# Splitting the first loads of a LayerNorm-MLP kernel over two DMA queues, and the first copy into two parts

## Chip, cores and metric

The kernel runs on 1 core of a Trainium2 chip. The metric is device time in microseconds for one execution of the whole program. Before the change three runs gave 396.62, 396.86 and 396.88 us; the median is 396.86 us.

## What is computed

```python
def _layernorm(x, axis=-1, eps=1e-5):
    m = jnp.mean(x, axis=axis, keepdims=True)
    v = jnp.var(x, axis=axis, keepdims=True)
    return (x - m) / jnp.sqrt(v + eps)

# B, S, D, F = 1, 2048, 1024, 3584; all inputs bfloat16
def reference(x, w1, b1, w2, b2):
    y = _layernorm(x, axis=-1)
    h = _gelu(jnp.einsum("bsd,df->bsf", y, w1) + b1)     # tanh approximation
    return jnp.einsum("bsf,fd->bsd", h, w2) + b2
```

## The kernel before

The 2048 rows of `x` are cut into 16 tiles of 128 rows, and four tiles make a block of 512 rows. For each block the kernel needs the normalized rows transposed (`yT_sb`, with the 1024 features in 8 groups of 128), then multiplies by `w1` (28 rows of 128 hidden features, 8 matmuls each), applies gelu on ScalarE into `hT_sb`, multiplies by `w2` and adds `b2` on VectorE. Blocks 1 to 3 are normalized and transposed on VectorE while TensorE works on the block before them.

Block 0 has nothing ahead of it to hide behind, so it is treated differently. Its first three tiles (`N_RAW = 3`) are transposed raw, that is, not yet normalized, by TensorE (`pe_T`, line 378): four transposes of 128x128 per half tile go to a PSUM bank, and ScalarE copies the bank to `yT_sb` (line 386). TensorE multiplies these raw values by the first 7 rows of `w1` (`cells`, through `pe_cell`, line 410), in the order that is written out by hand at lines 560 to 591: an order that follows the arrival of the loads. Meanwhile VectorE computes the statistics of each half tile (`op_stats`, line 269), from them the mean and the reciprocal deviation; these are turned into rows and spread over the partitions by GpSimd (line 497). VectorE then shifts the raw copies for the later rows of `w1` (`ops_fix`, line 334) and corrects the products of the first 7 rows in PSUM (lines 537 and 540). Only after that can ScalarE apply the first gelu and hand back the first PSUM bank to TensorE. Tile 3 is normalized before it is transposed (line 294).

VectorE's statistics run in a fixed order: first halves of tiles 0, 1, 2, then their second halves, then tile 3. The engines run separate instruction streams, each in the order in which the code puts it, and wait for one another by semaphores.

Ahead of all this TensorE does 24 dummy matmuls (`WARM`, line 486), and ScalarE loads the table for the square root (line 489).

The loads are issued from two queues. In the names of the first loads, `x0a` is the first half (512 columns) of tile 0; `xrb` is one transfer with the second halves of tiles 0 to 2 (384 KB); `w0` to `w7` are chunks of `w1` with 128 of the 1024 input features and the first 896 hidden features each (224 KB). ScalarE's queue carries `x1a` and `x2a`; all others are on SP's queue, in the order of `SP_FIRST_LOADS` (line 26). After the first loads SP issues the rest of `w1`, block 1 of `x`, `w2`, `b2` and the last two blocks.

Of the kernel before, what the change touches and what calls it, by code (L numbers as in the profile page):

```python
# [5 lines left out]
ACT = mybir.ActivationFunctionType  # L6
# [7 lines left out]
TPB = TB // P  # L14
# [5 lines left out]
WARM = 24  # L20
N_RAW = 3
RC = N_RAW * P
HALVES = (0, 4, 8)
W1_CHUNK_COLS = (512, 512, 1024, 640)
N_W2_CHUNKS = 4
SP_FIRST_LOADS = ("x0a", "w0", "w1", "w2", "xrb", "w3", "w4", "x3a", "x3b", "w5", "w6", "w7", "b1", "w8")
ACT_FIRST_LOADS = ("x1a", "x2a")

T_PE_START = 4.2
T_DVE_START = 26.0  # L30
# [54 lines left out]
def bass_standalone__mixer_channel_mlp__prompt_kernel(  # L85
# [13 lines left out]
    DT = D // P  # L99
# [6 lines left out]
    assert HC <= 512 and DT * P * 2 <= 2048 and FT >= 4 and FT <= P  # L106
    R = max(1, min(R_WAVE, FT - 2, NB1 + NB2))
    assert NB1 + NB2 + 1 <= 8 and NB2 == 2
    assert HALVES[-1] == DT and 0 < N_RAW < TPB

    w1_chunks = [(j, j + 1, 0, R * P) for j in range(DT)]
    c0 = R * P
# [24 lines left out]
    with ExitStack() as es:  # L137
# [34 lines left out]
        act = _Prog("s_act")  # L172
# [7 lines left out]
        x_ev = {}  # L180
        w1_issued = set()

        def dma(dst, src, sig, nbytes, waits=()):
            dma_q[0].op(lambda e, dst=dst, src=src: e.dma_start(dst, src), waits=waits, sig=sig, sem="d_" + sig, inc=16)
            dma_bytes[0] += nbytes
            est[sig] = DMA_T0 + dma_bytes[0] / DMA_BYTES_PER_US

        def load_x_tile(i):
            dma(x_sb[:, i, :], xf[i * P:(i + 1) * P, :], f"x{i}", P * D * 2)
            x_ev[i] = (f"x{i}", f"x{i}")  # L190
# [7 lines left out]
        def load_w1(ci):  # L198
            j0, j1, a, b = w1_chunks[ci]
            dma(w1_sb[:, j0:j1, a:b], w1v[:, j0:j1, a:b], f"w1c{ci}", (j1 - j0) * P * (b - a) * 2)  # L200
            w1_issued.add(ci)
# [5 lines left out]
        def issue(item):  # L207
            if item == "xrb":
                dma(x_sb[:, 0:N_RAW, HC:D], xf[0:N_RAW * P, HC:D].rearrange("(t p) d -> p t d", p=P), item,
                    N_RAW * P * HC * 2)  # L210
                for i in range(N_RAW):
                    x_ev[i] = (f"x{i}_0", item)
            elif item[0] == "x" and item[-1] in "ab":
                i, h = int(item[1:-1]), "ab".index(item[-1])
                dma(x_sb[:, i, h * HC:(h + 1) * HC], xf[i * P:(i + 1) * P, h * HC:(h + 1) * HC], f"x{i}_{h}",
                    P * HC * 2)
                x_ev[i] = (f"x{i}_0", f"x{i}_1")
            elif item == "b1":
                b1v = b1.rearrange("(t q a) -> q t a", q=4, a=32)
                for q in range(4):  # L220
                    dma(b1r_sb[32 * q:32 * q + FT, :], b1v[q], f"b1{q}", F // 2, waits=["b1z"])
            elif item[0] == "x":
                load_x_tile(int(item[1:]))
            elif item[0] == "w" and int(item[1:]) < len(w1_chunks):
                load_w1(int(item[1:]))

        dma_q[0] = act
        for item in ACT_FIRST_LOADS:
            issue(item)
        dma_q[0] = sp  # L230
        for item in SP_FIRST_LOADS:
            issue(item)
        for i in range(TPB):
            if i not in x_ev:
                load_x_tile(i)
            else:
                for h, evn in enumerate(x_ev[i]):
                    if evn not in est:
                        issue(f"x{i}" + "ab"[h])
# [10 lines left out]
        for b in range(2, NB):  # L250
# [5 lines left out]
                waits=["ones"], sig="ident")  # L256
# [11 lines left out]
        def op_stats(i, h):  # L268
            return (lambda e, i=i, h=h: e.bn_stats(st_sb[:, i, 6 * h:6 * (h + 1)], x_sb[:, i, h * HC:(h + 1) * HC]),  # L269
                    [x_ev[i][h]], f"st{i}_{h}", 0.65)  # L270

        def op_aggr(i):
            if i >= TPB:
                pool.op(lambda e, i=i: e.tensor_tensor(out=rstd_sb[:, i:i + 1], in0=mv_sb[:, i, 1:2],  # L274
                                                       in1=nhalf[:, i:i + 1], op=ALU.pow),
                        waits=[f"mv{i}", "nhalf"], sig=f"rstd{i}")
            return (lambda e, i=i: e.bn_aggr(mv_sb[:, i, :], st_sb[:, i, :]),  # L277
                    [f"st{i}_0", f"st{i}_1", "eps"], f"mv{i}", 0.33)
# [20 lines left out]
        y_ev = {}  # L299
# [32 lines left out]
        def ops_fix(i):  # L332
            s0, s1 = i * P, (i + 1) * P
            return [(lambda e: e.tensor_tensor(out=yT_sb[:, 0, :, s0:s1], in0=yT_sb[:, 1, :, s0:s1],  # L334
                                               in1=row_sb[:, 0:1, s0:s1].to_broadcast([P, DT, P]), op=ALU.add),
                     ["row0", f"te{i}_0", f"te{i}_1"], f"fx{i}v", 1.25)]

        yT_ev = {}
        mm1_done = {}
# [19 lines left out]
        def dve_put(o):  # L359
            dve.op(o[0], waits=o[1], sig=o[2])  # L360
# [4 lines left out]

        def pe_T(parts, bname):
            bap = t_bank[bname]
            nb = HALVES[1]
            last = f"tp{parts[-1][0]}_{parts[-1][1]}"
            w0 = ["ident"] + ([bank_read[bname]] if bname in bank_read else [])  # L370
            copies = []
            for n, (i, k) in enumerate(parts):
                j0, j1 = HALVES[k], HALVES[k + 1]
                buf, s0 = (1 if i < N_RAW else 0), i * P
                o = n * nb * P
                for j in range(j0, j1):
                    waits = (w0 if n == 0 else []) + [x_ev[i][k] if i < N_RAW else y_ev[i][j]] if j == j0 else []
                    pe.op(lambda e, i=i, j=j, o=o + (j - j0) * P: e.transpose(  # L378
                        out=bap[:, o:o + P], in_=x_sb[:, i, j * P:(j + 1) * P], identity=ident[:, :]),
                        waits=waits, sig=(f"tp{i}_{k}" if j == j1 - 1 else None))  # L380
                    yT_ev.setdefault(i, [None] * DT)[j] = f"te{i}_{k}"
                src = bap[:, o:o + (j1 - j0) * P].rearrange("p (j s) -> p j s", j=j1 - j0)
                copies.append((yT_sb[:, buf, j0:j1, s0:s0 + P], src, f"te{i}_{k}"))
                pe_t[0] += (j1 - j0) * 0.056
            for dst, src, sig in copies:
                act.op(lambda e, dst=dst, src=src: e.copy(out=dst, in_=src), waits=[last], sig=sig)  # L386
                bank_read[bname] = sig
# [96 lines left out]
        def warm(n, gate=None):  # L484
            for _ in range(n):
                pe.op(lambda e: e.matmul(ps_1[:, 0, 0:P], lhsT=unit, rhs=unit,  # L486
                                         start=True, stop=True), waits=[gate] if gate else [])

        act.op(lambda e: e.preload_act_table(ACT.Sqrt))
        warm(WARM)  # L490
        raw = list(range(N_RAW))
        head = [op_stats(i, h) for h in range(2) for i in raw] + [op_aggr(i) for i in raw]
# [3 lines left out]
        for k in range(2):  # L496
            pool.op(lambda e, k=k: e.partition_broadcast(
                row_sb[:, k, 0:RC], rvt_sb[0:1, k * N_RAW:(k + 1) * N_RAW, :].rearrange("p v s -> p (v s)")),
                waits=["rvt", "row1c", "scr"], sig=f"row{k}")
        pool.op(lambda e: e.tensor_tensor(out=scr_sb[:, 1, :], in0=scr_sb[:, 0, :], in1=nhalf[:, :], op=ALU.pow),  # L500
                waits=["row1"])
        h = DT // 2
        FX = [f"fx{i}v" for i in raw]
        for i in raw:
            head += ops_fix(i)
        for o in head:
            dve_put(o)

# [3 lines left out]
        def cells(rows, dts, t0, t1, by_row=False):  # L512
            n0, n1 = t0 * P, t1 * P + (1 if t1 == N_RAW else 0)
            order = [(r, dt) for r in rows for dt in dts] if by_row else [(r, dt) for dt in dts for r in rows]
            for r, dt in order:
                bank = wave[r][0]
                w = [yT_ev[i][dt] for i in range(t0, t1)] + (["rone"] if n1 > RC else [])
                if r not in started:
                    w += [bank_read[k] for k in (f"{bank[0]}_{bank[1]}",) if k in bank_read]
                pe_cell(r, dt, 1, n0, n1, bank, w, f"cw_{r}" if dt == DT - 1 and n1 > RC else None,  # L520
                        r not in started, False, shared=True)
                started.add(r)
# [26 lines left out]
        def late_cells(t, rows, dts):  # L549
            for r in rows:  # L550
# [7 lines left out]
                        hT_row[(0, r)] = f"g_0_{r}"  # L558

        first, most, every = range(NB1), [*range(NB1), R - 1], range(R)  # L560
        pe_T([(0, 0)], "t")
        pe_T([(1, 0)], "2_0")
        cells(first, (0,), 0, 1)
        pe_T([(2, 0)], "2_1")
        cells(first, (0,), 1, 2)
        cells((R - 1,), (0,), 0, 2)
        cells(most, (1,), 0, 2)
# [4 lines left out]
        cells(every[4:], (2,), 0, 3)  # L572
        cells(first, (3,), 0, 3)
        pe_T([(2, 1)], "t")
        cells(every[NB1:], (3,), 0, 3)
        act.op(lambda e: e.activation(out=std_sb[:, :], in_=mv_sb[:, 0:TPB, 1], func=ACT.Sqrt, bias=0.0, scale=1.0),
               waits=[f"mv{i}" for i in range(TPB)], sig="std")
# [52 lines left out]
        while ci < len(crit) or fi < len(fill):  # L630
# [5 lines left out]
            if take_crit:  # L636
                rdy, o, _ = crit[ci]
                ci += 1
            else:
                rdy, o, _ = fill[fi]  # L640
# [46 lines left out]
```

## Time and profile before

| | before |
|---|---|
| median of 3 runs | 396.86 us (396.62 to 396.88) |
| profiled execution, its own time | 397.14 us |
| its span | 395.9 us |
| TensorE matmul busy | 393.0 us (99%) |
| VectorE busy | 160.1 us (40%) |
| ScalarE busy | 83.7 us (21%) |
| DMA, mean over the span | 60 GB/s |
| DMA, first five of the 40 slices of the span | 256 to 388 GB/s |

The span is the time from the first to the last instruction of the program in the profiled execution; the execution's own time has 1.24 us around it. In the profile PE is TensorE's matmuls, PEld its weight loads, DVE is VectorE, ACT is ScalarE, POOL is GpSimd and SP is SyncE. A name with q (ACTq, SPq) is the engine's sequencer, which issues DMAs. L386 is line 386 of the kernel. Matmul records overlap, since matmuls are pipelined: the distance of two starts says more than the length of one record. In chains of waits each piece is given with its start and its length in us; in timelines the bracket at the end gives the engine's idle time before the piece and what ended it.

### The profile page before, as it was taken

The page shows a single profiled execution, that of the slowest core. Times are in us where ns is not written, and L with a number is a line of the kernel's source. Part 1 is how long each engine was busy: PE and PEld are TensorE (multiplying, and loading weights), DVE is VectorE, ACT ScalarE, POOL GpSimd, SP SyncE. Part 2 cuts the span into 40 slices and gives each one's busy share as a digit, 9 for nine tenths or more (in the row PEclk, how much of TensorE's full clock was granted, in tenths as well). Part 3 has the DMA queues.
Part 4 walks back from the last instruction along what each step waited for, and adds up shares of the span by engine and source line. Part 5 has one row for each costly group of instructions (what it writes and reads, how often), then busy time and mean ns, then how long its engine had stood idle before and what let it go on. Part 6 is the DMA issues. An engine that isn't in the chain of part 4 may idle for free.

```text
span 395.9 us, 4579 instructions
## 1 busy us (share of the span) xinstructions
PE 393.0 (99%) x1964; PEld 186.6 (47%) x1964; DVE 160.1 (40%) x336; ACT 83.7 (21%) x125; POOL 11.9 (3%) x28
## 2 busy tenths in 40 slices
PE   8999999999999999999999999999999999999998
PEld 7744444444444444444444444444444444444445
DVE  4998889988999405987100000001100000001011
ACT  3374330000144342000023443100003334400000
POOL 0121100011000100000000000000000000000000
DMA  7999940000000000000000000000000000000000
GB/s 256 365 378 387 388 167 14 28 26 14 28 0 0 2 0 2 27 17 24 26 13 2 0 0 2 13 13 28 21 21 13 0 2 0 0 15 26 13 28 27
DMA packets 16747, 23.62 MB, mean 60 GB/s; under 512 B 1240, under 2 KB 10456, under 8 KB 16728
## 3 DMA queue, kind: packets, MB, share of 16 engines
q1 hardware_dynamic: 16440, 23.08, 16.6%
q8 instruction: 15, 0.25, 0.3%
q10 hardware_dynamic: 288, 0.26, 0.2%
q14 instruction: 4, 0.03, 0.0%
HBM read 19.14 MB, written 4.19 MB: 59 GB/s over the span
## 4 chain that ended last, share of the span: by engine, by line
PE 99%; ACT 0%; DVE 0%; issue 0%
PE ps L462 49%; PE ps L410 41%; PE ps_t L410 8%; PE ps L486 1%; PE ps_t L378 0%; ACT yT_sb L386 0%; PE ps L378 0%; DVE o_sb L473 0%
## 5 line engine op out<-in xcount | busy, mean ns | idle before, releaser
L462 PE MATMUL ps<-w_sb,hT_sb 128*128 128x512 bf16 (+2 forms) x924 | 194.1, 373 | 0.0
L410 PE MATMUL ps<-yT_sb,w_sb 128*128 128x512 bf16 (+4 forms) x832 | 167.1, 360 | 0.3 <-ACT yT_sb L386 0.3
L462 PEld LDWEIGHTS ps<-w_sb,hT_sb 128*128 128x128 bf16 x924 | 89.3, 98 | 104.5
L410 PEld LDWEIGHTS ps<-yT_sb,w_sb 128*128 128x128 bf16 x832 | 78.1, 98 | 84.8 <-ACT yT_sb L386 0.5
L419 ACT ACTIVATE hT_sb<-ps,b_sb 128x512 bf16<-128x512 f32 x94 | 64.2, 688 | 235.6 <-PE ps L410 217.2
L473 DVE TENSOR_TENSOR o_sb<-ps,b_sb 128x512 bf16<-128x512 f32 (+2 forms) x33 | 22.3, 676 | 198.5 <-PE ps L462 198.4
L354 DVE STREAM_TRANSPOSE yT_sb<-x_sb 32x256 bf16<-32x256 bf16 x192 | 83.7, 436 | 21.6 <-PE ps_t L410 18.6
L410 PE MATMUL ps_t<-yT_sb,w_sb 128*128 128x512 bf16 (+2 forms) x152 | 34.0, 368 | 0.0
L269 DVE BATCH_NORM_STATS2 st_sb<-x_sb 128x6 f32<-128x512 bf16 x32 | 21.1, 674 | 6.0 <-DMA x_sb<-in_x_dram 5.8
L410 PEld LDWEIGHTS ps_t<-yT_sb,w_sb 128*128 128x128 bf16 x152 | 14.5, 98 | 16.4
L419 ACT ACTIVATE hT_sb<-ps_t,b_sb 128x512 bf16<-128x512 f32 x18 | 12.4, 687 | 18.0 <-PE ps_t L410 14.6
L545 DVE TENSOR_TENSOR ps<-ps,row_sb 128x384 f32<-128x384 f32 x17 | 9.3, 564 | 3.1 <-PE ps L410 2.7
L274 POOL TENSOR_TENSOR rstd_sb<-mv_sb,nhalf 128x1 f32<-128x1 f32 x12 | 6.5, 542 | 99.6 <-DVE mv_sb L277 99.6
L294 DVE TENSOR_SCALAR x_sb<-x_sb,mv_sb,rstd_sb 128x1024 bf16<-128x1024 bf16 x13 | 7.0, 541 | 1.9 <-POOL rstd_sb L274 1.3
L386 ACT COPY yT_sb<-ps_t 128x512 bf16<-128x512 bf16 x6 | 3.3, 587 | 4.9 <-PE ps_t L378 4.9
L537 DVE SCALAR_TENSOR_TENSOR ps<-row_sb,cs_sb,ps 128x385 f32<-128x385 f32 x7 | 4.3, 615 | 0.0
L540 DVE TENSOR_TENSOR ps<-ps,row_sb 128x385 f32<-128x385 f32 x7 | 4.0, 568 | 0.2
L277 DVE BATCH_NORM_AGGREGATE mv_sb<-st_sb 128x2 f32<-128x15 f32 x16 | 3.3, 214 | 1.2
L334 DVE TENSOR_TENSOR yT_sb<-yT_sb,row_sb 128x1024 bf16<-128x1024 bf16 x3 | 3.7, 1293 | 0.0
L486 PE MATMUL ps<-const-bfloat16-1.0 128*128 128x128 bf16 x24 | 2.7, 312 | 0.8 <-PEq L672 0.8
L500 POOL TENSOR_TENSOR scr_sb<-scr_sb,nhalf 128x16 f32<-128x16 f32 x1 | 2.9, 2947 | 8.4 <-issue 8.4
L486 PEld LDWEIGHTS ps<-const-bfloat16-1.0 128*128 128x128 bf16 x24 | 2.5, 148 | 0.8 <-issue 0.8
(33 smaller groups left out, 18.7 us busy)
## 6 DMA issues: line engine op xcount, KB each, us to landing
w_sb<-in_w_dram SPq DMA_DIRECT2D x4, 1792.0 KB, 18.1
out_dram<-o_sb SPq DMA_DIRECT2D x31, 128.0 KB, 1.7
x_sb<-in_x_dram SPq DMA_DIRECT2D x3, 1024.0 KB, 14.0
w_sb<-in_w_dram SPq DMA_DIRECT2D x2, 1024.0 KB, 9.2
w_sb<-in_w_dram SPq DMA_DIRECT2D x1, 2048.0 KB, 15.2
w_sb<-in_w_dram SPq DMA_DIRECT2D x8, 224.0 KB, 5.7
w_sb<-in_w_dram SPq DMA_DIRECT2D x1, 1280.0 KB, 16.3
x_sb<-in_x_dram SPq DMA_DIRECT2D x3, 128.0 KB, 5.6
```

What stands on the lines that cost most here:

```text
L269: return (lambda e, i=i, h=h: e.bn_stats(st_sb[:, i, 6 * h:6 * (h + 1)], x_sb[:, i, h * HC:(h + 1) * HC]), [x_ev[i][h]], f"st{i}_{h}", 0.65)
L274: pool.op(lambda e, i=i: e.tensor_tensor(out=rstd_sb[:, i:i + 1], in0=mv_sb[:, i, 1:2], in1=nhalf[:, i:i + 1], op=ALU.pow), waits=[f"mv{i} ...
L294: return (lambda e, i=i, c0=c0, c1=c1: e.tensor_scalar(out=x_sb[:, i, c0:c1], in0=x_sb[:, i, c0:c1], scalar1=mv_sb[:, i, 0:1], scalar2=rst ...
L354: res.append((lambda e, src=src, dst=dst: e.transpose(out=dst, in_=src), waits, (f"tr{i}" if lastop else None), 0.47))
L410: pe.op(lambda e: e.matmul(unit_bank(bank)[:, n0:n1], lhsT=w1_sb[:, dt, r * P:(r + 1) * P], rhs=yT_sb[:, buf, dt, n0:n1], start=start, sto ...
L419: act.op(lambda e, r=r, n0=n0, n1=n1, bank=bank: e.activation(out=hT_sb[:, r, n0:n1], in_=unit_bank(bank)[:, n0:n1], func=ACT.Gelu_apprx_tanh,
L462: pe.op(lambda e, st=st, ft=ft, c0=c0, c1=c1, bank=bank: e.matmul(ps_2[:, bank, 0:c1 - c0], lhsT=hT_sb[:, ft, st * P:(st + 1) * P], rhs=w2 ...
L473: crit.append((est[sig], (lambda e, ob=ob, c0=c0, c1=c1, bank=bank: e.tensor_tensor(out=o_sb[:, ob, c0:c1], in0=ps_2[:, bank, 0:c1 - c0], ...
L486: pe.op(lambda e: e.matmul(ps_1[:, 0, 0:P], lhsT=unit, rhs=unit, start=True, stop=True), waits=[gate] if gate else [])
L537: return [(lambda e: e.scalar_tensor_tensor(out=ap, in0=row_sb[:, 0, :], scalar=cs_ap[r], in1=ap, op0=ALU.mult, op1=ALU.add), [f"m1_0_{r}" ...
L540: (lambda e: e.tensor_tensor(out=ap, in0=ap, in1=row_sb[:, 1, :], op=ALU.mult), [f"sa_{r}", "row1"], f"sb_{r}", 0.56)]
L545: crit.append((est[wait_ev], (lambda e: e.tensor_tensor(out=ap, in0=ap, in1=row_sb[:, 1, 0:RC], op=ALU.mult), [wait_ev, "row1"], f"sc_{r}" ...
```

## The change

Four things are edited.

1. The load `w1` (the second chunk of the weights, input features 128 to 255) and `xrb` are issued from ScalarE's queue, behind `x1a` and `x2a`, and no longer from SP's.
2. ScalarE's load of the square-root table is put behind the issue of `x1a`, ahead of the other three issues; before, it stood behind both.
3. The first half of tile 0 is transposed and copied in two parts of two transposes each (parts 2 and 3 of `PARTS`), each to a bank of its own, and the copies are 128x256 and no longer 128x512. Tiles 1 and 2 move to the next banks (`2_1` and `t`).
4. For that, the events that the copies signal are looked up by feature group, and `ops_fix` is called further down in the program text, when all copies are known; its instructions keep their place in VectorE's order.

```diff
-HALVES = (0, 4, 8)
+PARTS = ((0, 4), (4, 8), (0, 2), (2, 4))
-SP_FIRST_LOADS = ("x0a", "w0", "w1", "w2", "xrb", "w3", "w4", "x3a", "x3b", "w5", "w6", "w7", "b1", "w8")
-ACT_FIRST_LOADS = ("x1a", "x2a")
+SP_FIRST_LOADS = ("x0a", "w0", "w2", "w3", "w4", "x3a", "x3b", "w5", "w6", "w7", "b1", "w8")
+ACT_FIRST_LOADS = ("x1a", "x2a", "w1", "xrb")
...
         for item in ACT_FIRST_LOADS:
             issue(item)
+            if item == "x1a":
+                act.op(lambda e: e.preload_act_table(ACT.Sqrt))
...
-                     ["row0", f"te{i}_0", f"te{i}_1"], f"fx{i}v", 1.25)]
+                     ["row0"] + list(dict.fromkeys(yT_ev[i])), f"fx{i}v", 1.25)]
...
-                j0, j1 = HALVES[k], HALVES[k + 1]
+                j0, j1 = PARTS[k]
...
-                    waits = (w0 if n == 0 else []) + [x_ev[i][k] if i < N_RAW else y_ev[i][j]] if j == j0 else []
+                    waits = (w0 if n == 0 else []) + [x_ev[i][j // nb] if i < N_RAW else y_ev[i][j]] if j == j0 else []
...
-        act.op(lambda e: e.preload_act_table(ACT.Sqrt))
         warm(WARM)
...
-        for i in raw:
-            head += ops_fix(i)
...
-        pe_T([(0, 0)], "t")
-        pe_T([(1, 0)], "2_0")
+        pe_T([(0, 2)], "t")
+        pe_T([(0, 3)], "2_0")
+        pe_T([(1, 0)], "2_1")
         cells(first, (0,), 0, 1)
-        pe_T([(2, 0)], "2_1")
+        pe_T([(2, 0)], "t")
         cells(first, (0,), 1, 2)
...
         pe_T([(2, 1)], "t")
+        for i in raw:
+            for o in ops_fix(i):
+                dve_put(o)
```

More of the change, by code (lines that the diff above doesn't have):

```diff
@@ L108, in bass_standalone__mixer_channel_mlp__prompt_kernel @@
     assert NB1 + NB2 + 1 <= 8 and NB2 == 2
-    assert HALVES[-1] == DT and 0 < N_RAW < TPB
+    assert PARTS[1][1] == DT and 0 < N_RAW < TPB
     w1_chunks = [(j, j + 1, 0, R * P) for j in range(DT)]
@@ L216, in issue @@
                     P * HC * 2)
-                x_ev[i] = (f"x{i}_0", f"x{i}_1")
+                x_ev[i] = (f"x{i}_0", x_ev[i][1] if i in x_ev else f"x{i}_1")
             elif item == "b1":
@@ L367, in pe_T @@
             bap = t_bank[bname]
-            nb = HALVES[1]
+            nb = DT // 2
             last = f"tp{parts[-1][0]}_{parts[-1][1]}"
```

## Prediction

> **What bounds the kernel now.** I read the page first, then the chain of waits over the first microseconds, then the timeline of each engine there, and last the DMA stretch by stretch. The page:
>
> ```profile
> span 395.9 us, 4579 instructions
> ...
> PE 393.0 (99%) x1964; PEld 186.6 (47%) x1964; DVE 160.1 (40%) x336; ACT 83.7 (21%) x125; POOL 11.9 (3%) x28
> ...
> q1 hardware_dynamic: 16440, 23.08, 16.6%
> ...
> q10 hardware_dynamic: 288, 0.26, 0.2%
> ```
>
> TensorE leaves 2.9 of 395.9 us, so only the start can gain anything. q10 is ScalarE's queue: it carries just the 0.26 MB of x1a and x2a; q1 is SP's. The chain over the first 9 us:
>
> ```profile
> 0.83 2.72 PE ps L486 x24
> 3.54 0.55 PE ps_t L378 x4
> ...
> 4.12 0.59 ACT yT_sb L386
> 4.72 0.05 issue
> 4.76 0.72 PE ps L410 x5
> ...
> 8.79 0.22 PE ps_t L378 x4
> ```
>
> After the 24 warm-up matmuls come the transposes of tile 0, then the only non-TensorE link: the copy of tile 0's half, for which the first product waits. In the records of single matmuls the last transpose of x1a starts at 4.20 and, at the 107 ns of its neighbours, is through by 4.31; the first product starts at 4.76: a hole of 0.46 us. From 5.7 us on consecutive starts fit the column counts up to the end. Matmuls start 107 ns apart up to 6.05 us and 56 ns apart after it (128 columns), though the granted clock reads 1.00 throughout.
>
> A second chain runs beside TensorE, from the second halves (`xrb`) through VectorE to the first gelu:
>
> ```profile
> 8.18 1.88 DVE L269 BATCH_NORM_STATS2 st_sb<-x_sb 128x6 f32<-128x512 bf16 x3 [2.69 <-DMA x_sb<-in_x_dram]
> ...
> 11.73 0.11 DVE L281 TENSOR_SCALAR rv_sb<-mv_sb 128x3 f32<-128x3 f32 x1
> ...
> 15.19 3.73 DVE L334 TENSOR_TENSOR yT_sb<-yT_sb,row_sb 128x1024 bf16<-128x1024 bf16 x3
> 18.85 0.61 DVE L537 SCALAR_TENSOR_TENSOR ps<-row_sb,cs_sb,ps 128x385 f32<-128x385 f32 x1
> ```
>
> VectorE has idled 2.69 us for `xrb` (issued 2.64, 5.5 us to land: 8.16), and from then to the first correction it has only short gaps for ScalarE's square root (0.33) and GpSimd's broadcast. The first gelu starts at 20.09 and takes 0.69. TensorE's weight load waits for it:
>
> ```profile
> 20.83 0.14 PEld L410 LDWEIGHTS ps<-yT_sb,w_sb 128*128 128x128 bf16 x2 [0.18 <-ACT hT_sb L419]
> ```
>
> Its matmul starts at 20.87, just when the one before is through. So this chain has about 0.04 us of slack: whatever delays `xrb` by more reaches the end. The next gelus come 1.125 us apart and a row of matmuls takes 1.73, so it stalls TensorE once.
>
> Last, the DMA while both queues had work (3.28 to 4.21), and then SP's alone:
>
> ```profile
> 3.28:4.21 0.93, 0.93 (x11) 0.74 (x8) 0.82 (x2) 0.09 (x1) 0.00 (x0) 1.00 1.00 355
> 4.25:5.40 1.15, 0.90 (x10) 0.64 (x8) 1.03 (x2) 0.95 (x2) 0.00 (x0) 1.00 0.96 335
> 5.40:7.05 1.65, 1.65 (x18) 1.57 (x17) 0.09 (x1) 0.58 (x1) 0.00 (x0) 1.00 0.93 261
> ```
>
> ```profile
> q1 hardware_dynamic: 128, 0.20, 60.0%
> q10 hardware_dynamic: 139, 0.13, 39.9%
> ```
>
> The last two columns of the first are DMA share and GB/s; the second is the queues' part of 3.28 to 4.21. The engines were full (1.00), and the two queues moved about the same number of packets: they took turns.
>
> **The change, part by part.** *Copy of tile 0 in two parts.* Transposes and products stay the same in number and order. A 128x512 copy takes 0.585 us, the 128x5 copy of line 528 0.165, hence 0.83 ns per column and an estimated 0.37 us for 128x256. The copy before began 0.35 us after the start of the last transpose; two transposes earlier, this is 3.96, and its end 4.33 instead of 4.71. But the product also needs w0, which landed at 4.60, and nothing ahead of w0 moves. A transpose followed the landing of x0a (3.36) by 0.14 us, so the product starts at 4.66 to 4.74: 0.02 to 0.1 us earlier. The extra copy (two of 0.37 for one of 0.585) delays nothing: the copy of tile 1 can't start before its transposes, about 4.55, and before it started at 4.60. I count 0.03 us of gain. Banks: `2_0`, `2_1` and `t` are handed on at copies that end before their next user needs them. The fixes keep their place in VectorE's order, so moving their code costs nothing.
>
> *Table load ahead of x2a, w1 and xrb.* It takes 1.28 us, ended at 2.99 before and would end by 2.5; the first copy needs it at about 4. In this trace a sequencer runs on beside its busy engine (VectorE's takes a wait at 15.21, inside the fix that began at 15.19), so I cost the issues behind it at nothing: x2a at about 1.2, w1 at 1.7, xrb at 2.1. If they wait for it instead, each is 1.28 later (a rival below).
>
> *w1 and xrb on ScalarE's queue.* SP loses two issues of 0.47 us each, so w2, w3, w4 and x3 enter q1 earlier and lie there with data ready. From 4.25, when x2a is through, q10 holds w1 and xrb, and q1 holds w2, w3, w4, x3a, x3b. By turns:
> - w1 has 128 packets of 1792 B (0.229 MB), and as many of w2 and w3 pass beside it: 0.459 MB at 355 GB/s is 1.29 us, so the last packet at 5.54; before, 4.69. w1 lands 0.85 later, at 6.8 instead of 5.97. TensorE needs it at 6.31: a stall of about 0.5.
> - xrb has 384 packets of 1 KB, and 384 of q1 go with them: some 220 of 1792 B (rest of w3, w4), 164 of 1 KB (x3a, part of x3b). Together 0.955 MB, 2.69 us, to 8.23; before, 7.05. xrb lands 1.18 later, at 9.34.
>
> That rate is from the one stretch with the same mix, hence my choice. Ends: the best long stretch of this trace, 365 GB/s between 9.2 and 12 us and 395 in its best part, gives at 390 a delay of 0.83; xrb's own 261 GB/s, with 335 for w1, gives 2.2. A gain in landing has no row for it while turns are taken; it stands as a rival.
>
> The Trainium skill bears on this: "DMA: Bandwidth & Descriptors", section "Rules for kernel authors", says that spreading DMAs over issuing engines doesn't raise bandwidth, since all share 16 engines, and only saves issue time. Held to one-queue rows (335 and 261, a mean of 291 over 4.25 to 7.05) the delay would be about 2.1 us; the 355 of both queues lies above these but below the 365 that SP's queue reached later, so the trace doesn't contradict it.
>
> TensorE then reaches the second transposes (8.63 before, behind xrb) at about 9.1 and waits to about 9.45. VectorE starts its second halves 1.18 later, with x3 landed by then, and nothing in its chain shortens: gelu 0 ends 1.18 later, where 0.04 is slack. TensorE's stalls at w1, at the transposes and at gelu 0 are parts of this one delay and not added to it. Sum: +1.14 for xrb, -0.03 for the copy already hidden behind it: **+1.1 us**. The profiled execution took 397.14 (span 395.9 and 1.24 around it) and becomes 398.3; it lay 0.28 above the median, which becomes 396.86 + 1.14 = **398.0**.
>
> **Rivals.** *Not slower: q10 keeps its early place.* If q10's packets pass ahead of q1's backlog, w1 follows x2a at 4.25 and takes 0.64 us, and xrb takes 1.08 to 1.65 us, ending at 6.0 to 6.5: a landing 0.5 to 1 us earlier. Then the chain to gelu 0 is free, and TensorE gains at most its 0.46 us hole: 396.4 to 396.8, say 396.6. It decides from the point where xrb lands by 8.2. For it: SP's issue time of 0.47 per load is indeed saved. Against it: 128 and 139 packets in the same stretch.
>
> *The table load holds the queue.* x2a, w1 and xrb are issued 1.28 us later (2.5, 2.95, 3.4). w0, now alone, lands sooner, and x2a by turns at about 5.3 to 5.6, where TensorE wants it by 5; w1's last packet comes about 6.1 and xrb's about 8.6, since q1 has used the time: xrb 1.5 us late, 398.3. The split of the load is then not what the change says. Against it: the wait taken at 15.21.
>
> *The clock steps up late.* If holes at w1 keep the matmuls at 107 ns spacing, the 2.3 us of work between 6.31 and 8.63 takes 4.6, from 6.8 to 11.4, and TensorE is 2.8 us late: 399.6. For it: the step at 6.05 came after one hole of 0.46. Against it: the step comes before the stall at w1. The Trainium skill, "TensorE: Matmul & The Clock Gate", section "What's actually happening", lets the clock rise after one busy window and fall only after an idle one of about 3.4 us; no hole foreseen here is as long.
>
> **How the numbers follow.** By turns 0.71, q10 early 0.15, table load holding 0.10, late clock 0.04. 0.2% is 0.79 us, about what a measurement of this kernel can tell from no change. In the first case the bounds +0.8 to +2.2 give 397.6 to 399.1, and perhaps 0.08 of its 0.71 falls under the 0.79 by yet faster transfers. Of the second nearly all lies within 0.2%, since more than 0.79 us would need the step at 6.05 some 1.6 us earlier too: 0.03. Faster 0.03, same 0.20, slower 0.77. The range goes from 396.9, leaving out most of the second case, to 399.2.
>
> **What would show it.** Right: xrb lands at 9 to 10, VectorE's first second half starts there (8.18 before), TensorE idles near 6.3 and ahead of the second transposes, LDWEIGHTS waits for gelu 0, and everything from 21 us on is shifted by the same 1.1. The copies of tile 0 take 0.37, and the first product starts at 4.7, with w0. Wrong: xrb landing by 8.2, or w1 before 6.3; ScalarE's issues only from 2.5 on would point to the table load; a spacing of 107 ns beyond 7 us to the clock.

## Result and profile after

The changed kernel takes 398.57 us (median of 17 runs, 397.46 to 402.23) against 396.97 us before (17 runs beside it, 396.59 to 397.51): 1.60 us more. The ratio, estimated from all runs, is 1.0052, with a 95% interval of 1.0037 to 1.0068 (the two medians alone give 1.0040; the ratios below are estimated in the same way). The forecast was 398.0, from 396.9 to 399.2.

Single executions lie much further apart than before. Eleven of the 17 had a mean granted TensorE clock of 1.000 and took 397.46 to 398.93 us; six had 0.996 or 0.991 and took 399.70 to 402.23. The profiled one is of the second kind, the slowest of all (402.23, span 401.0); a typical one follows behind it. Its page, the lines that answer to those of before and the row of granted clock, which the page of before doesn't have:

```profile
span 401.0 us, 4581 instructions
...
PE 394.8 (98%) x1964; PEld 187.7 (47%) x1964; DVE 160.2 (40%) x336; ACT 83.8 (21%) x126; POOL 12.0 (3%) x28
...
PEclk8799999999999999999999999999999999999999
...
q1 hardware_dynamic: 15896, 22.46, 15.9%
q10 hardware_dynamic: 832, 0.88, 0.7%
```

ScalarE's queue (q10) now carries 0.88 MB. The chain of waits of the same execution over the first 26 us:

```profile
1.71 6.98 DMA w_sb<-in_w_dram
8.70 0.05 issue
8.74 4.69 PE ps L412 x26
13.43 0.85 PE ps_t L380 x8
```

w1 is issued at 1.71 and lands at 8.70; TensorE, ready for it at about 5.5, stands still. Then the products run at half rate up to about 14, and in them 8 transposes take 0.85 us where they took 0.45 before. The table by stretches (columns as before, granted clock third from the right) shows when it fell:

```profile
6.50:7.00 0.50, 0.00 (x0) 0.00 (x0) 0.00 (x0) 0.00 (x0) 0.00 (x0) 1.00 1.04 317
7.00:7.50 0.50, 0.00 (x0) 0.00 (x0) 0.00 (x0) 0.00 (x0) 0.00 (x0) 0.82 1.01 338
7.50:8.00 0.50, 0.00 (x0) 0.00 (x0) 0.00 (x0) 0.00 (x0) 0.00 (x0) 0.50 1.00 302
...
13.00:14.00 1.00, 1.00 (x10) 0.83 (x9) 1.00 (x6) 0.00 (x0) 0.00 (x0) 0.50 1.10 346
14.00:15.00 1.00, 1.00 (x9) 0.67 (x8) 1.00 (x2) 0.69 (x2) 0.00 (x0) 0.93 1.10 350
```

0.82 over 7.0 to 7.5 puts the fall at about 7.3, some 1.8 us into the hole; the clock came back shortly after 14. So about 6.8 us of this execution ran at half clock, which gives the mean of 0.991; a mean of 0.996 is, by the same sum, about 3 us at half clock.

The 16 increments of w1's semaphore, as many as the core has DMA engines (I read them as one from each), arrive in this trace between 5.78 and 6.50 us for 13 engines and at 7.70, 8.34 and 8.70 for the last three: a few late engines make the whole landing late. They were late in sending: the last of w1's 128 packets starts at 8.06 (at 5.67 in the typical execution below), and one that started at 4.55 took 1.25 us, where the median is 0.07. Why they were late is not shown.

None of the first set's executions with a clock of 1.000 has a trace. A typical execution is that of the changed kernel's second set of runs (`e5_again` below: 398.28 median; the profiled one 398.18, span 396.9). Its VectorE timeline:

```profile
9.22 1.88 DVE L271 BATCH_NORM_STATS2 st_sb<-x_sb 128x6 f32<-128x512 bf16 x3 [3.46 <-DMA x_sb<-in_x_dram]
...
12.77 0.10 DVE L283 TENSOR_SCALAR rv_sb<-mv_sb 128x3 f32<-128x3 f32 x1
...
16.23 3.73 DVE L336 TENSOR_TENSOR yT_sb<-yT_sb,row_sb 128x1024 bf16<-128x1024 bf16 x3
19.88 0.61 DVE L536 SCALAR_TENSOR_TENSOR ps<-row_sb,cs_sb,ps 128x385 f32<-128x385 f32 x1
```

and the weight load that waits for the first gelu:

```profile
21.87 1.19 PEld L412 LDWEIGHTS ps<-yT_sb,w_sb 128*128 128x128 bf16 x7 [0.60 <-ACT hT_sb L421]
```

Every entry of VectorE's chain stands 1.03 to 1.04 us later than before (8.18, 11.73, 15.19, 18.85), the gelu ends at 21.82 instead of 20.78, and the span is 1.04 longer. All that this execution lost is the lateness of `xrb`.

### The profile page after: what moved, and what is told of

It is laid out like the page before. It is cut to its first block, busy times and chain, and to the rows that moved or that the text cites. A ratio compares the mean times of both kernels' runs of the same rounds, so it can differ in the third digit from the quotient of the medians.

```text
span 401.0 us, 4581 instructions
## 1 busy us (share of the span) xinstructions
PE 394.8 (98%) x1964; PEld 187.7 (47%) x1964; DVE 160.2 (40%) x336; ACT 83.8 (21%) x126; POOL 12.0 (3%) x28
## 3 DMA queue, kind: packets, MB, share of 16 engines
q1 hardware_dynamic: 15896, 22.46, 15.9%
## 4 chain that ended last, share of the span: by engine, by line
PE 97%; DMA 2%; ACT 0%; ACTq 0%; DVE 0%; issue 0%
PE ps L464 48%; PE ps L412 41%; PE ps_t L412 8%; DMA w_sb<-in_w_dram 2%; PE ps_t L380 0%; ACT L231 0%; ACTq L184 0%; DVE o_sb L475 0%
## 5 line engine op out<-in xcount | busy, mean ns | idle before, releaser
L412 PE MATMUL ps<-yT_sb,w_sb 128*128 128x512 bf16 (+4 forms) x832 | 169.0, 363 | 3.5 <-DMA w_sb<-in_w_dram 3.5
L412 PEld LDWEIGHTS ps<-yT_sb,w_sb 128*128 128x128 bf16 x832 | 79.0, 100 | 88.7 <-DMA w_sb<-in_w_dram 3.3
L388 ACT COPY yT_sb<-ps_t 128x512 bf16<-128x512 bf16 (+1 forms) x7 | 3.7, 557 | 11.1 <-PE ps_t L380 11.1
```

The costliest lines, as they stand in the source:

```text
L412: pe.op(lambda e: e.matmul(unit_bank(bank)[:, n0:n1], lhsT=w1_sb[:, dt, r * P:(r + 1) * P], rhs=yT_sb[:, buf, dt, n0:n1], start=start, sto ...
```

## Experiments

All differences lie within a few us at the start, so for most I give the landings of w1 and xrb in the profiled execution beside the time. A landing is one execution's; two tables at the end of this section put them side by side. Only differences from the changed kernel or the one before are shown.

**Only the split copy** (loads and table load as before):

```diff
-SP_FIRST_LOADS = ("x0a", "w0", "w2", "w3", "w4", ...
+SP_FIRST_LOADS = ("x0a", "w0", "w1", "w2", "xrb", "w3", "w4", ...
-ACT_FIRST_LOADS = ("x1a", "x2a", "w1", "xrb")
+ACT_FIRST_LOADS = ("x1a", "x2a")
-            if item == "x1a":
+            if item == "x2a":
```

> Only the copy of tile 0 in two parts; all loads and the table load as before the change. Theory (taking turns: the loss is all in the loads): xrb lands at about 8.2 us as before, the copies of tile 0 take 0.37 us each, the first product starts at 4.65 to 4.74 instead of 4.76, held by w0; time within 0.1 us of 396.97. Rival (the split copy itself costs, by one more ScalarE instruction and other banks): slower by 0.3 us or more with xrb unmoved.

Measured: 396.89 against 397.04 us, ratio 0.9995 (0.9986 to 1.0004): no difference. A line each of the timelines of ScalarE, of TensorE's matmuls and of its weight loads:

```profile
3.79 0.37 ACT L388 COPY yT_sb<-ps_t 128x256 bf16<-128x256 bf16 x1 [0.81 <-PE ps_t L380]
```

```profile
4.72 0.44 PE L412 MATMUL ps<-yT_sb,w_sb 128*128 128x128 bf16 x5 [0.63 <-DMA w_sb<-in_w_dram]
```

```profile
20.53 0.55 PEld L412 LDWEIGHTS ps<-yT_sb,w_sb 128*128 128x128 bf16 x4 [0.58 <-ACT hT_sb L421]
```

The copy takes 0.37 us, and the product, free since about 4.2, waits for w0: the copy bought 0.04 us. In this execution the matmuls were 56 ns apart already at 3.5 us, and TensorE was through with its work ahead of the first reused bank at 20.17 instead of 20.87; half of these 0.7 us went into waiting for the gelu, since xrb (7.85) was just 0.3 earlier. So the second chain is a bound of its own.

**Only the loads**, copy in one part, table load behind all four issues:

```diff
-SP_FIRST_LOADS = ("x0a", "w0", "w1", "w2", "xrb", "w3", ...
-ACT_FIRST_LOADS = ("x1a", "x2a")
+SP_FIRST_LOADS = ("x0a", "w0", "w2", "w3", ...
+ACT_FIRST_LOADS = ("x1a", "x2a", "w1", "xrb")
...
-                x_ev[i] = (f"x{i}_0", f"x{i}_1")
+                x_ev[i] = (f"x{i}_0", x_ev[i][1] if i in x_ev else f"x{i}_1")
```

The last edit, which the changed kernel has too, only keeps xrb as the event of the second halves when it is issued before `x0a`.

> Only w1 and xrb moved to ScalarE's queue; the copy is in one part and the table load stands behind all four issues. Theory: the whole loss is here: 398.2 to 398.9 (the changed kernel 398.57), w1 landing at 6.5 to 8.7, xrb at 9 to 11.7, single runs spread over some us with a mean clock under 1.00 in the slowest. Rival (the table load's new place or the split copy has a part in it): faster than the changed kernel by 0.4 us or more.

Measured: 398.24 (397.98 to 398.58, 6 runs) against 397.04 us, ratio 1.0032 (1.0020 to 1.0045); w1 at 6.34, xrb at 9.01. The loss is in the loads. The narrow spread and a clock of 1.000 in all six were not as expected; six runs are few, though.

**One of the two moved.** First the changed kernel with xrb back on SP's queue:

```diff
-SP_FIRST_LOADS = ("x0a", "w0", "w2", "w3", ...
-ACT_FIRST_LOADS = ("x1a", "x2a", "w1", "xrb")
+SP_FIRST_LOADS = ("x0a", "w0", "w2", "xrb", "w3", ...
+ACT_FIRST_LOADS = ("x1a", "x2a", "w1")
```

> The changed kernel with xrb back on SP's queue behind w2; only w1 is added to ScalarE's queue. Theory: w1 takes turns with w2 and xrb and lands at 6.5 to 7 (5.97 before), a stall of 0.3 to 0.7 us at the first w1 product; w2 and xrb swap no bytes with it in total, so xrb lands within 0.3 us of 8.16 and the end shifts by 0 to 0.5 us: 397.0 to 397.5. Rival (it is w1's late landing that sets the time, by the hole in TensorE's work): +1 us or more, 398 or more.

Measured: 397.81 us, ratio 1.0017 (1.0009 to 1.0026), between theory and rival. w1 landed at 7.17, xrb at 8.09 (8.16 before), and TensorE idled 1.3 us ahead of the first w1 product. This execution took 398.06 us, one of the slower ones; its span was 396.8, and no weight load waited for the gelu: here TensorE's own chain was the later one. w1 alone on the second queue costs 0.8 us, more than I expected.

Then the changed kernel with w1 back on SP's queue:

```diff
-SP_FIRST_LOADS = ("x0a", "w0", "w2", "w3", ...
-ACT_FIRST_LOADS = ("x1a", "x2a", "w1", "xrb")
+SP_FIRST_LOADS = ("x0a", "w0", "w1", "w2", "w3", ...
+ACT_FIRST_LOADS = ("x1a", "x2a", "xrb")
```

> The changed kernel with w1 back on SP's queue; only xrb is added to ScalarE's queue. Theory: xrb starts at 4.3 on ScalarE's queue, in turns with w1, w2, w3: w1 lands at about 6.5, xrb's 384 packets go with 384 of SP's (w1, w2, w3: 0.688 MB), 1.08 MB at 355 GB/s from 4.25, to 7.3, and xrb lands at about 8.4: 397.0 to 397.6. Rival (any transfer of many packets on the second queue is held up by SP's backlog for as long as in the changed kernel): xrb at 9.3 or later and 398 or more.

Measured: 397.26 us, ratio 1.0006 (0.9997 to 1.0015). xrb landed at 7.58, 0.8 ahead of my estimate and 0.6 ahead of before, and w1 at 5.62. Taking turns from 4.3 on, xrb overtakes SP's w3 (8.68) and makes w2 later (7.36, 6.54 before); in these runs it became late only where w1 stood ahead of it in the same queue. Its earliness brought nothing: TensorE's clock rose at 6.4 us in this execution, and its own chain set the end.

**The changed kernel again**, on the chip of the next three:

> The changed kernel itself, unchanged, on the same chip as the next three. Theory: w1 and xrb land late by taking turns, and when the hole at w1 is long the clock granted to TensorE falls back: median 398.2 to 398.9, w1 landing at 6.3 to 8.7, xrb at 9 to 11.7, single executions spread over more than 1 us, those with a mean clock under 1.000 being the slowest. Rival (the long holes belong to the chip of the first runs): spread under 0.7 us as in the kernel with only the loads moved (397.98 to 398.58), no execution with a clock under 1.000.

Measured: 398.28 (398.03 to 399.23, 7 runs) against 397.14 us, +1.14 us, ratio 1.0037 (1.0023 to 1.0052). w1 landed at 6.26, xrb at 9.19. The spread is over 1 us, but no run had a clock under 1.000. What makes some executions have the late DMA engines of the first profile stays open. The queues from 4.25 to 8.30 us, while both had work, and in the part from 5.6 to 8.3, when q10 carried mostly xrb:

```profile
q1 hardware_dynamic: 512, 0.75, 56.0%
q10 hardware_dynamic: 519, 0.59, 43.9%
```

```profile
q1 hardware_dynamic: 350, 0.49, 57.1%
q10 hardware_dynamic: 381, 0.38, 43.7%
```

and the rates of the stretches:

```profile
4.30:5.60 1.30, 0.84 (x10) 0.64 (x8) 0.94 (x2) 0.86 (x3) 0.00 (x0) 1.00 0.98 349
5.60:8.30 2.70, 2.70 (x34) 2.59 (x33) 0.16 (x1) 0.59 (x1) 0.00 (x0) 1.00 1.01 321
```

Turns by packets again, at 321 to 349 GB/s: as many packets of each queue, whatever their size.

**The table load behind all four issues:**

```diff
-            if item == "x1a":
+            if item == "xrb":
```

> The changed kernel with the table load behind all four of ScalarE's issues. Theory (the table load's place is worth nothing, since the issues run on beside it): the same as the changed kernel within 0.3 us. Rival (the table load beside the issues is what delays the landing of w1 in the slow executions): 398.0 to 398.6 with a narrow spread, as with only the loads moved.

Measured: 398.43 us (397.66 to 399.90, 12 runs), ratio 1.0032 (1.0021 to 1.0043), as the changed kernel. One run had a clock of 0.996 and took 399.90, and the spread is wide, so the table load's place isn't the reason for the slow executions either. The profiled one, 398.83, is the second slowest: w1 landed at 7.47 and xrb at 9.83, and VectorE's chain began 1.68 us later than before and the span was 1.69 longer, with a clock of 1.000. That the issues run on beside it is seen in ScalarE's timeline of the changed kernel:

```profile
1.23 1.28 ACT L231 ACT_TABLE_LOAD   x1 [1.23 <-PEq L675]
1.26 0.42 ACTq L184 DMA_DIRECT2D x_sb<-in_x_dram  x1
1.71 0.45 ACTq L184 DMA_DIRECT2D w_sb<-in_w_dram  x1
2.19 0.46 ACTq L184 DMA_DIRECT2D x_sb<-in_x_dram  x1
```

**No backlog on SP's queue**, by a wait on SP ahead of w2:

```diff
         for item in SP_FIRST_LOADS:
+            if item == "w2":
+                sp.op(None, waits=["w1c1"])
             issue(item)
```

> The changed kernel with SP's queue held behind w0 until w1 has landed, so w1 and most of xrb have the DMA engines to themselves. Theory (turns): w1 lands at 5.3 to 6.0 and xrb at 7.2 to 8.0, earlier than before the change; w2 is issued at about 5.6 and lands at 7.8 to 8.7, and TensorE, which wants it at about 7.9, waits up to 0.8 us for it; time 396.9 to 397.8, under the changed kernel by 0.7 us or more. Rival (ScalarE's queue is slow by itself, without a backlog on SP's): w1 at 6.3 or later, xrb at 9 or later, time 398.2 or more.

Measured: w1 at 5.65, xrb at 6.62, both earlier than before the change (xrb even by 0.6 us more than expected) and far from the 6.3 to 8.7 and 9.2 to 11.7 of the changed kernel. VectorE's timeline, and the rate once w1 and most of xrb were through (last column):

```profile
6.64 1.88 DVE L273 BATCH_NORM_STATS2 st_sb<-x_sb 128x6 f32<-128x512 bf16 x3 [1.07 <-DMA x_sb<-in_x_dram]
```

```profile
5.60:6.60 1.00, 1.00 (x13) 0.84 (x11) 0.00 (x0) 0.48 (x1) 0.00 (x0) 1.00 0.18 60
```

So ScalarE's queue isn't slow: what holds it is the other queue's backlog. The time, 398.11 us (397.54 to 401.61, ratio 1.0034, 1.0018 to 1.0050), is no better, and I had expected 397.8 at most: the wait empties SP's queue, the DMA moves 60 GB/s between 5.6 and 6.6 us, and TensorE then waits for the later weights, 3.5 us in all for three of them in the profiled execution. That one is the slowest, 401.61 us with a clock of 0.996; what a typical execution lost has no trace. In it the matmuls fell back to half rate at about 14.9, 0.4 us after a hole of 2.4 us had ended.

**A load that nobody needs early on the second queue**, the rest as before the change:

```diff
-SP_FIRST_LOADS = (... "w2", "xrb", "w3", "w4", ...
-ACT_FIRST_LOADS = ("x1a", "x2a")
+SP_FIRST_LOADS = (... "w2", "xrb", "w4", ...
+ACT_FIRST_LOADS = ("x1a", "x2a", "w3")
```

> The kernel before with nothing changed but that w3 is issued from ScalarE's queue behind x2a; w1, w2 and xrb stay on SP's. w3 isn't needed before about 9.6. Theory (turns): w3's 128 packets pass beside w1's, so w1 lands at 6.2 to 6.8 instead of 5.97, w2 and xrb 0.5 to 0.7 us later than before (xrb 8.6 to 8.9), w3 2 us earlier; time +0.3 to +0.8 us: 397.3 to 397.8. Rival (only a transfer that sits on ScalarE's queue is slow): w1, w2 and xrb unmoved, time within 0.1 us of before.

Measured: 397.56 against 397.14 us, ratio 1.0017 (1.0008 to 1.0026). w1 landed at 6.40 (5.97 before) and w2 at 6.93 (6.54), though they hadn't been touched; w3 at 6.58 (8.88); xrb at 8.29, only 0.13 later. Landings scatter, though: with w1, w2, w3 and xrb all on SP's queue, w1 landed at 5.34, 5.97 and 6.09 in three executions. The second table below is surer: the middle of w1's 16 increments came at 5.70, against 5.04 to 5.14 in those three, and that of xrb's at 7.94, against 6.91 and 7.10. So untouched loads do become later, as the theory has it; xrb's last increment hides it. In the profiled execution (clock up at 6.7, no wait for the gelu) TensorE's own chain set the end; how the 0.42 divides between the loads and the clock isn't shown.

**Two tries at a faster order.** One queue again, split copy as in the changed kernel, xrb ahead of w2 (the order is shown against the one before):

```diff
-SP_FIRST_LOADS = ("x0a", "w0", "w1", "w2", "xrb", "w3", ...
+SP_FIRST_LOADS = ("x0a", "w0", "w1", "xrb", "w2", "w3", ...
```

> The split copy, the table load behind both issues, and one SP queue as before except that xrb is issued ahead of w2. Theory (the first 512-column product can't start before the second halves' statistics plus 12.66 us, and otherwise TensorE's own chain with its varying clock step decides): xrb lands at 6.9 to 7.6, its chain frees, w2 lands at 7.4 to 8.2 where TensorE wants it at 7.3 to 8.0; executions in which the clock opens early gain up to 0.4 us, the others nothing or lose 0.3 at w2: median 396.6 to 397.1. Rival (order within one queue moves nothing): xrb within 0.2 us of 8.16 and the time within 0.1 us of before.

Measured: 397.07 against 397.02 us, ratio 1.0000 (0.9991 to 1.0009). xrb landed at 7.13, a full us earlier, w2 at 7.72; the time is the same. In this execution w1 landed at 6.09 and cost TensorE 0.5 us.

And w0 ahead of all on SP's queue, for the first hole:

```diff
-SP_FIRST_LOADS = ("x0a", "w0", "w2", "w3", ...
-ACT_FIRST_LOADS = ("x1a", "x2a", "w1", "xrb")
+SP_FIRST_LOADS = ("w0", "x2a", "w1", "w2", "xrb", "w3", ...
+ACT_FIRST_LOADS = ("x0a", "x1a")
```

> The changed kernel with x0a and x1a on ScalarE's queue and w0 first on SP's, then x2a, w1, w2, xrb, w3 and on there as before. Theory: w0 lands at 3.8 to 4.3, the first product starts at 4.4 to 4.6 instead of 4.76 (the transposes of tile 1 now wait for x1a), w1, w2 and xrb as before within 0.3 us, and since xrb's chain sets the end when TensorE is early, the median moves by no more than 0.2 us: 396.8 to 397.2. Rival (the first hole is what counts): 396.7 or less.

Measured: 399.37 us, ratio 1.0050 (1.0037 to 1.0064): a clear miss. The profiled execution is the slowest of five, 400.24. In it w0 landed at 4.86, not by 4.3, and x0a, in turns with it, at 5.01 instead of 3.36; xrb landed at 8.67, 0.5 later. TensorE's first transposes began 1.7 us later, and after that hole its matmuls stayed 107 ns apart until 10.97 us. How the 2.35 us divide between x0a and the half rate was not separated.

No version here beats the kernel before.

**The two chains in one table.** When the matmuls' starts go from 107 to 56 ns apart ("clock up at"; in the row with a range a hole hides it), start of the second halves' statistics, end of gelu 0, whether the weight load waits for it, and the span, from the profiled executions:

| kernel | clock up at | statistics | gelu 0 ends | weight load waits, us | span |
|---|---|---|---|---|---|
| before | 6.2 | 8.18 | 20.78 | 0.18 | 395.91 |
| only the copy | by 3.5 | 7.88 | 20.48 | 0.58 | 395.58 |
| only the loads | 4.8 | 9.03 | 21.63 | 0.59 | 396.76 |
| changed, again | 6.4 | 9.22 | 21.82 | 0.60 | 396.95 |
| table load last | 6.2 to 7.5 | 9.86 | 22.46 | 0.60 | 397.60 |
| w1 moved | 5.4 | 8.11 | 21.09 | no | 396.82 |
| xrb moved | 6.4 | 7.60 | 20.28 | no | 395.89 |
| w3 moved | 6.7 | 8.31 | 20.91 | no | 396.19 |
| xrb ahead of w2 | by 3.6 | 7.16 | 20.14 | no | 395.75 |

Where the weight load waits, the span less the start of the statistics is 387.70 to 387.74 us in all five, while that start moves by 1.98 us. So there the end follows xrb alone. Where it doesn't wait, it is 387.9 to 388.7, and TensorE's own chain (its clock step and its holes at w1) sets the end.

**The landings taken apart.** A load counts as landed with the last of its semaphore's 16 increments. The middle of the 16 (mean of the 8th and 9th) and the last, in us:

| kernel | w1 middle | w1 last | xrb middle | xrb last |
|---|---|---|---|---|
| before | 5.04 | 5.97 | 7.10 | 8.16 |
| only the copy | 5.10 | 5.34 | 6.91 | 7.85 |
| w3 moved | 5.70 | 6.40 | 7.94 | 8.29 |
| only the loads | 5.85 | 6.34 | 8.31 | 9.01 |
| changed, again | 5.95 | 6.26 | 8.31 | 9.19 |
| table load last | 5.84 | 7.47 | 8.10 | 9.83 |
| changed, first set (slowest) | 6.09 | 8.70 | 8.21 | 11.74 |

With both loads moved the middles agree within 0.25 us, in the slowest execution too, and stand 0.7 to 1.1 us after before for w1 and 1.0 to 1.4 for xrb, counting both executions of the old order. The last increments scatter by 2.4 and 2.7 us. So turns account for the middle, and the scatter of the engines comes on top of it.

## Why the prediction held, and where it didn't

- *xrb's delay reaches the end less 0.04.* Held: 1.04 late at the statistics, 1.04 at the end in the typical execution; a slack of 0.04 is too small to see. The sum +1.14 meets the +1.14 of the second set of runs; the first set had +1.60. Of that set the eleven executions with a clock of 1.000 have a median of 398.38, +1.41; without a trace of one, it isn't shown how much of this is a later xrb.
- *Turns by packets between the queues.* Held (512 against 519 packets), and shown by taking the backlog away: xrb at 6.62. The estimate of 9.34 for xrb stands against 9.01, 9.19 and 9.83 in the three ordinary executions, but 11.74 in the slowest. That 9.34 lies so near is partly luck. The 355 GB/s were 349 and 321, so xrb's last packet started at 8.72 and not at 8.23; but it landed 0.47 after that, where I had carried over 1.11. That 1.11 was too long because, by the count of 1 KB packets, xrb before ran to about 7.7, not 7.05.
- *w1 at 6.8.* Measured 6.3 to 8.7. The mis-sized term is the time from the last packets to the landing, which I carried over unchanged. It is set by the slowest of the 16 increments: before, 15 of w1's 16 increments were there by 5.20 and the last came at 5.97; in the typical execution all 16 came between 5.63 and 6.26; in the slowest, three came 1.2 to 2.2 us after the other 13. By the middle of the increments w1 came 0.80 to 1.05 later than before, against the 0.85 forecast. The stragglers, and not the mean rate, make the times spread upward. The foreseen stall of 0.5 at w1 was nothing in the typical execution, where TensorE had started its products later because w0 landed at 4.86; the foreseen wait ahead of the second transposes, 0.35, was 0.39.
- *The copy.* 0.37 us, product held by w0: the first product started at 4.62 in the changed kernel's first profile and at 4.72 with the copy alone, no measurable time. Held. (Two transposes earlier is 3.91 by the single starts, not 3.96; as w0 decides, nothing hangs on it.)
- *Table load beside the issues.* Held; that rival is out.
- *Not slower, q10 early.* Out by the packet counts. Had xrb come early, it would have brought nothing by itself: at 7.13 to 7.6 the time stayed that of before.
- *Clock late, 0.04.* This was too small, and the form was wrong. I took the step at 6.05 (by the single starts it is 6.2) as a constant; in the table of the two chains it lies between 3.5 and 6.7 where it can be read closely. And in the first set's profiled execution the clock did not come late behind the hole but fell in it. Six of that set's 17 executions show a mean clock under 1.000, and these are the slowest six; that the other five fell in a hole at w1 as well is likely but not shown. My reason against it leaned on the Trainium skill, "TensorE: Matmul & The Clock Gate", section "What's actually happening", by which the clock falls after an idle window of about 3.4 us. In the trace it fell 1.8 us into a hole of 3.2 us, with another of 0.5 us shortly ahead of it, and in the run with SP's queue held back after a hole of 2.4 us; the measurement decides, and a hole need not be 3.4 us long.

## What to carry to other kernels

A second DMA queue brought little bandwidth here (between 4.25 and 8.30 us 304 to 318 GB/s with these loads on one queue, 330 or 331 with both moved, 307 in the slowest execution), but it changed the order: two queues with work take turns by packets, so moving urgent loads to the other queue lets less urgent ones pass beside them, unless the first queue has nothing left to send. Before moving a load, find each consumer's slack; here two chains, TensorE's and VectorE's, ended within 0.04 us of each other, so a gain in one was swallowed by the other and a loss in either came through. Price a late load by the slowest DMA engine, not by the mean rate, and a hole on TensorE by the clock as well.

## What the runs showed of the hardware that I had not expected

- In the slowest execution one landing was 2.2 us later than 13 of its 16 engines' parts (8.70 against 6.50), though the middle of the 16 came about when it did in the other executions (6.09 against 5.84 to 5.95).
- The step of the matmuls from 107 to 56 ns apart varied from execution to execution, 3.5 to 6.7 us with the first matmul at 0.8, and with a 1.8 us hole behind the warm-up it came between 10.97 and 11.24.
- The granted clock fell to 0.50 about 1.8 us into a hole, and matmuls then stayed at half rate for another 5.3 us of work; in another run it fell 0.4 us after a hole of 2.4 us had ended.
- The first weights' chunk (224 KB), issued first on SP's queue, landed at 4.86 us, while the first 128 KB of `x`, issued ahead of it, landed at 3.3 to 3.4 in the other runs; side by side on two queues the same `x` needed until 5.01.
